# One mask instruction for four heads, and the transfer of the negated maxima asked for by GpSimd

## The chip, the cores and the metric

The kernel runs on one core of a Trainium2 chip. The metric is the device time of one execution in microseconds (us), the median over several runs. The core's engines are TensorE (PE, its weight loads shown apart as PEld), VectorE (DVE), ScalarE (ACT), GpSimd (POOL) and SyncE (SP), which here only asks for DMA transfers. Each engine takes its own instructions in order and waits on semaphores for the others.

## The reference

A block of 2048 tokens of width 512 is normalised and goes through two branches: attention in a sliding window of 256 over 32 heads of 16, and a SwiGLU feed-forward of width 1792. The feed-forward's result, through another silu, gates the attention's.

```python
def _A_ref(x, wqkv, wo):
    B, S, D = x.shape
    H = 32; Dh = D // H; W = 256
    qkv = (x @ wqkv).reshape(B, S, 3, H, Dh).transpose(2, 0, 3, 1, 4)
    q, k, v = qkv[0], qkv[1], qkv[2]
    scores = jnp.einsum("bhqd,bhkd->bhqk", q, k) * (Dh ** -0.5)
    idx = jnp.arange(S)
    mask = (idx[:, None] - idx[None, :] >= 0) & (idx[:, None] - idx[None, :] < W)
    p = softmax(jnp.where(mask[None, None], scores, -1e9))
    o = jnp.einsum("bhqk,bhkd->bhqd", p, v)
    return o.transpose(0, 2, 1, 3).reshape(B, S, D) @ wo

def _B_ref(x, w_gate, w_up, w_down):
    return (silu(x @ w_gate) * (x @ w_up)) @ w_down

xn = layernorm(A_x)
out = A_x + _A_ref(xn, A_wqkv, A_wo) * silu(_B_ref(xn, B_w_gate, B_w_up, B_w_down))
```

All tensors are float32.

## The kernel before, in words

**Precision and the two halves.** A float32 operand is split into a high part (names ending in `h`, written by ACT) and the remainder (names ending in `l`, written by POOL or DVE), and a product is the sum of three matmuls (`PAIRS`). A matmul uses 64 rows of the array, so two streams run side by side: half 0 on rows 0 to 63, half 1 on rows 64 to 127. `next_mm` gives each half its next matmul.

**Dense work.** Tokens come in 4 chunks (`NCH`) of 512. Per chunk there are units of dense work: `Proj` (`a`, queries and keys of two groups of heads), `Values` (`vp`), `GateUp` (`g`, `u`), `Down` (`d`) and `Wo` (`s`). Each has its weights loaded by SP into `wr` (two buffers), split by ACT into `wh` (L429) and by POOL into `wl` (L434), with three buffers each. All dense matmuls are at L470.

**Attention.** 32 units, 8 groups of four heads in each chunk. The four heads of a unit are two pairs `p` of one head `h` in either half of the rows. A unit's steps:

- `load_qk`: queries and keys go through DRAM (`qkd`) into `qs` and `ks`.
- `max_pair`: the scores `b` by query row (L970); DVE takes each row's maximum over the window (L978) into `m`.
- `max_turn`: PE transposes the maxima into `mt` (L1004); ACT negates them into `ms`, 16 x 128 (`neg`, L1019). A transfer of 8 KB (`put`) writes them into `qs` as a 49th row, so that the next product subtracts the maximum.
- `prob_pair(u, e, p)`: for one pair of heads and one set `e` of key blocks (`pieces`: three sets in the first chunk, four later) the transposed scores `c` (L1121), the exponential by ACT into `t`, a part of the buffer `p` (L1082), and on the blocks that the window's edge crosses a mask by POOL: L1095 on the diagonal, L1099 at the far edge. Each set has two such blocks. There are 480 masks in all, of 2 heads x 128 columns.
- `pv_visit`: the product with the values (L1158), once a unit when all its sets are masked; then `ev`, `od`, the denominators, and `o` for `Wo`.

**What sets the order.** The order of instructions on every engine is worked out when the kernel is built, by a planner that runs its own clock. `do(engine, ready, cost, fn, then, slack)` puts an instruction in a list, and `pump` issues from each list the one with the smallest `ready + slack`; `V`, `S`, `G` and `D` are DVE, ACT, POOL and the transfers that SP asks for (`dma`). A transfer's planned end is that of a stream of 230 KB/us plus `LAND` = 3.5 us, and at most eight are under way. `streams` holds the attention's steps with due marks counted in units of dense work: the maxima from u + 0.02, their transposition at u + 0.8, the probabilities from u + 1.07 in steps of 0.1, the product with the values at u + 1.89. A step is issued when it is due and its readiness function (`prob_ready`, `pv_ready`) gives a time that has come; otherwise PE gets dense matmuls. `prob_ready` asks for `ms_at[u]`, the planned arrival of the negated maxima, and for two PSUM banks; `pv_ready` asks for `pt_at`, the planned end of the masks.

`p_take` gives out pieces of the buffer `p` (`PCAP` = 6784 columns) in a ring; a unit's pieces are free again when its `pv_visit` is issued.

Of the kernel before, what the change touches and what calls it, by code (L numbers as in the profile page):

```python
# [13 lines left out]
ALU = mybir.AluOpType  # L14
# [3 lines left out]
P = 128  # L18
# [37 lines left out]
def tile_window_attention_swiglu_gate(  # L56
# [10 lines left out]
    nc = tc.nc  # L67
# [16 lines left out]
    def sb(name, shape, dtype, kind, n):  # L84
        return pers.tile(shape, dtype, name=name, tag=ring(kind, n), bufs=1)

    def f32(ap):
        return ap.bitcast(F32)

    def move(dst, src, eng=nc.sync):  # L90
        if dst.dtype == F32R:
            dst = f32(dst)
        if src.dtype == F32R:
            src = f32(src)
        eng.dma_start(dst, src)  # L95
# [11 lines left out]
    def do(e, ready, cost, fn, then=None, slack=0.5, can=None, lat=None):  # L107
        seq[0] += 1
        queue[e].append((ready + slack, seq[0], ready, cost, fn, then, can, LAT.get(e, 0.0) if lat is None else lat))
# [5 lines left out]
    def dma(ready, fn, then=None, slack=0.5, kb=256, can=None, e="D"):  # L115
        def begun_at(t):
            stream_at[0] = max(stream_at[0], t) + kb / 230.0
            done = stream_at[0] + LAND
            lanes.append(done)
            lanes.pop(0)  # L120
            if then:
                then(done)

        do(e, ready, 0.5, fn, begun_at, slack, lambda: lanes[0] <= now[0] and (can is None or can()), 0.0)
# [48 lines left out]
    def bank_time(pool, n=1):  # L173
        t = sorted(v for v in pool.values() if v is not None)
        return t[n - 1] if len(t) >= n else None

    def bank(pool, name):
        tag = min((v, k) for k, v in pool.items() if v is not None)[1]
        pool[tag] = None
        return ps.tile([P, 512], F32, name=name, tag=tag, bufs=1), tag  # L180
# [5 lines left out]
    qs = [pers.tile([P, 2, TC], F32R, name=f"q{i}") for i in range(3)]  # L186
# [168 lines left out]
    def half(r):  # L355
        return slice(R * r, R * r + R)

    def latest(times):
        times = list(times)
        return None if any(t is None for t in times) else max(times)  # L360
# [105 lines left out]
    def handover(pb):  # L466
        nc.vector.tensor_copy(pers.tile([MW, 1], F32, name="ho", tag=ring("ho", 2), bufs=1), pb[:MW, 0:1])
# [457 lines left out]
    ms_at = {}  # L925
# [72 lines left out]
    def max_turn(u, r):  # L998
        if r == 0:
            mtp[u] = [*bank(rb_free, f"mt{u}"), None]  # L1000
        pb, tag, _ = mtp[u]

        def go():
            nc.tensor.matmul(  # L1004
                pb[:MW, R * r : R * r + R], mts[u % 2][half(r), :], ident[half(r), half(r)],
                is_transpose=True, start=True, stop=True,
            )

        if r == 0:
            def after(t):  # L1010
                mtp[u][2] = t

            extra[0].append((128, go, lambda t: do("V", t, 0.09, lambda: handover(pb), after, -1.0)))
            return
        box = []

        def neg():
            box.append(sb(f"ms{u}", [16, P], F32R, "ms", 2))
            nc.scalar.activation(box[0], pb[:16, :P], AF.Copy, scale=-1.0)  # L1019

        def after_neg(t):
            rb_free[tag] = t
            dma(t, put, lambda t: ms_at.__setitem__(u, t + 1.0), -3.0, 8)

        def put():
            move(qs[u % 3][48 : 113 : 64], box[0])

        extra[1].append((128, go, lambda t: do("S", t, 0.25, neg, after_neg, -1.0)))

    def pieces(c, e):
        if c == 0:
            return ([(3, 2, 256, 0, 128, 256), (2, 2, 256, 256, 256, 512)],
                    [(0, 0, 384, 0, 0, 384)], [(1, 1, 384, 0, 0, 384)])[e]
        return ([(3, 2, 256, 0, 128, 256), (-2, 0, 256, 256, 256, 384)],
                [(-1, 0, 256, 0, 0, 256), (2, 2, 256, 256, 256, 512)],
                [(0, 0, 384, 0, 0, 384)], [(1, 1, 384, 0, 0, 384)])[e]

    pt = {}  # L1040
    pt_at = {}

# [4 lines left out]
    def p_place(n):  # L1049
        for at in (p_next[0], 0):  # L1050
            if at + n <= PCAP and all(at + n <= a or b <= at for a, b, _ in p_live):
                return at
        return None

    def p_take(h, n, u):
        at = p_place(h * n)
        p_live.append((at, at + h * n, u))
        p_next[0] = at + h * n
        return pbuf[:, at : at + h * n].rearrange("p (h n) -> p h n", h=h)

    def prob_span(u, e):
        pcs = pieces(u // NG, e)
        return min(q[4] for q in pcs), max(q[5] for q in pcs)

    def prob_ready(u, e, p):
        a, b = prob_span(u, e)
        if p_place(2 * (b - a)) is None:
            return None
        return latest([ms_at.get(u), bank_time(rb_free, 2), p_freed[0]])

# [2 lines left out]
    def prob_pair(u, e, p):  # L1073
        c = u // NG
        pcs = pieces(c, e)
        a, b = prob_span(u, e)
        t = p_take(2, b - a, u)
        pt[u, e, p] = t, a
        left = [2]

        def exp(h, pc):
            nc.scalar.activation(t[:, h, :], pc[:, a:b], AF.Exp, scale=DH ** -0.5)  # L1082

        blocks = []
        for kb, qb, w, at0, v0, v1 in pcs:
            q0 = qb + (v0 - at0) // P
            for blk in range((v1 - v0) // P):
                if q0 + blk == kb or q0 + blk == kb + 2:
                    blocks.append((v0 + blk * P, q0 + blk == kb))

        def masks():
            for at, diagonal in blocks:
                s = t[:, :, at - a : at - a + P]
                if diagonal:
                    nc.gpsimd.affine_select(  # L1095
                        s, s, [[0, 2], [1, P]], ALU.is_ge, 0.0, base=0, channel_multiplier=-1
                    )
                else:
                    nc.gpsimd.affine_select(  # L1099
                        s, s, [[0, 2], [-1, P]], ALU.is_gt, 0.0, base=0, channel_multiplier=1  # L1100
                    )

        def after(tm, tag):
            rb_free[tag] = tm
            left[0] -= 1
            if left[0] == 0:
                if blocks:
                    do("G", tm, 0.36 * len(blocks), masks, lambda t: pt_at.__setitem__((u, e, p), t), 0.0)
                else:
                    pt_at[u, e, p] = tm  # L1110

        for h in range(2):
            r = R * h
            pc, tag = bank(rb_free, f"c{u}_{e}_{2 * p + h}")

            def finished(t, h=h, pc=pc, tag=tag):
                do("S", t, 0.06 + 0.00081 * (b - a), lambda: exp(h, pc), lambda t: after(t, tag), 0.0)

            for i, (kb, qb, w, at0, _, _) in enumerate(pcs):
                def go(i=i, k0=HALO + kb * P, qb=qb, w=w, at0=at0, r=r, pc=pc):  # L1120
                    nc.tensor.matmul(  # L1121
                        pc[:, at0 : at0 + w], ks[u % 3][r : r + 49, p, k0 : k0 + P],
                        qs[u % 3][r : r + 49, p, qb * P : qb * P + w],
                        start=(i == 0), stop=True, skip_group_check=True,
                    )

                extra[h].append((w, go, finished if i == len(pcs) - 1 else None))

    def pv_ready(u, es):
        t = latest(pt_at.get((u, e, p)) for e in es for p in range(2))  # L1130
        c, g = divmod(u, NG)
        if any(vheld.get(((4 * c + kb) % VT, g // 4)) != 4 * c + kb for kb in range(-2 if c else 0, 4)):
            return None
        return None if t is None else latest([t, bank_time(rb_free, 2)])
# [268 lines left out]
    while True:  # L1403
        now[0] = max(front[0], min(clock))
        while marks and marks[-1][0] <= work[0] / PACE - LEAD:
            _, fn, a = marks.pop()
# [12 lines left out]
        if not any(extra):  # L1419
            s = work[0] / PACE - LEAD  # L1420
            for st in sorted(streams, key=lambda st: st[-1][0] if st else 1e9):
                if not st:
                    continue
                due, need, fn, a = st[-1]
# [4 lines left out]
                t = need(*a)  # L1429
# [20 lines left out]
        if os.environ.get("VIRT"):  # L1450
            u, i = stream[min(pos[0], len(stream) - 1)]
# [40 lines left out]
```

## Time and profile before

| | |
|---|---|
| three runs | 873.17, 872.02, 869.25 us; median 872.02 |
| the profiled execution | 870.93 us, of it 869.2 us from the first to the last instruction |
| granted TensorE clock | 0.999 |
| bytes moved by DMA | 139.63 MB, mean 161 GB/s |
| transfers `q<-ms` | 32, of 8 KB each, asked for by SP |
| masks on POOL | 256 at L1095 and 224 at L1099 |

A row of a group reads: line, engine, operation, output <- inputs, shapes, count | busy us, mean ns of one | idle time of the engine before them and what ended it. A row of waits reads: who waited <- for whom: us in total, times, longest. A row of the windows gives for each engine the busy us and the number of instructions, then the granted clock, the DMA engines' share and GB/s. `SPq` is SP's queue of requests. Masks that follow each other overlap a little in the records, so the distance of their starts is shorter than the time of one.

### The profile page before, as it was taken

How to read it: one execution, taken by the hardware profiler on the slowest of the kernel's cores; microseconds unless marked ns; L12 is line 12 of the kernel's file. 1: busy time of each engine (PE TensorE's matmuls, PEld its weight loads, DVE VectorE, ACT ScalarE, POOL GpSimd, SP SyncE). 2: the span in 40 equal slices, each digit the busy share in tenths (PEclk: the TensorE clock that was granted, in tenths of full speed). 3: DMA queues.
4: the chain of work that ended last, by engine and by line, in shares of the span. 5: the costliest groups of instructions: out<-in, count | busy, mean ns of one | idle time of the engine just before them, and what ended most of it. 6: DMA issues, size and time to landing. Idle time of an engine off the chain costs nothing.

```text
span 869.2 us, 30153 instructions
## 1 busy us (share of the span) xinstructions
PE 858.0 (99%) x11960; PEld 789.8 (91%) x11960; DVE 486.0 (56%) x1627; ACT 506.2 (58%) x1074; POOL 638.1 (73%) x888
## 2 busy tenths in 40 slices
PE   9999999999999999999999999999999999999997
PEld 8799999898889899989999989898999989999897
DVE  4364466655646655666555765565655566554233
ACT  4355565555665567565576666665656765566532
POOL 6576575668796776767799695676758997769774
PEclk9999999999999999999999999999999999999999
DMA  5785855466877985664767897556657779744342
GB/s 141 192 197 124 222 117 162 116 173 167 198 160 187 253 182 115 141 158 109 202 140 194 219 229 171 124 149 143 174 129 185 154 171 217 167 124 112 108 123 78
DMA packets 69489, 139.63 MB, mean 161 GB/s; under 512 B 14546, under 2 KB 23250, under 8 KB 69348
## 3 DMA queue, kind: packets, MB, share of 16 engines
q1 hardware_dynamic: 69060, 137.18, 63.9%
q8 instruction: 94, 1.54, 0.8%
q10 hardware_dynamic: 288, 0.52, 0.2%
q14 instruction: 47, 0.39, 0.2%
HBM read 107.74 MB, written 29.62 MB: 158 GB/s over the span
## 4 chain that ended last, share of the span: by engine, by line
PE 87%; DMA 8%; POOL 2%; SPq 1%; DVE 1%; issue 1%; ACT 1%; DVEq 0%; ACTq 0%; POOLq 0%
PE d L470 17%; PE u L470 15%; PE g L470 15%; PE a L470 11%; PE pv L1158 8%; PE s L470 5%; PE c L1121 5%; PE vp L470 4%; PE b L970 4%; DMA wr<-wo 2%; DMA k<-qkd 1%; POOL wl L434 1%; DMA den<-od 1%; DMA qkd<-qkl 1%; SPq L95 1%; DMA wr<-wqk 1%
## 5 line engine op out<-in xcount | busy, mean ns | idle before, releaser
L434 POOL TENSOR_TENSOR wl<-wr,wh 128x512 fp32r<-128x512 f32 (+2 forms) x258 | 306.8, 1207 | 101.1 <-ACT wh L429 91.9
L978 DVE CUSTOM_DVE_ANT_0 jk<-b,maskb 128x384 bf16<-128x384 f32 (+2 forms) x512 | 271.8, 531 | 132.5 <-PE b L970 71.5
L1082 ACT ACTIVATE p<-c 128x384 f32<-128x384 f32 (+1 forms) x480 | 208.2, 490 | 105.1 <-PE c L1121 89.0
L470 PE MATMUL d<-wh,hh 64*128 64x256 f32 x1792 | 259.3, 278 | 0.0
L470 PEld LDWEIGHTS d<-wh,hh 64*128 64x128 f32 x1792 | 227.1, 185 | 0.9 <-issue 0.6
L470 PE MATMUL d<-wl,hh 64*128 64x256 f32 x896 | 207.8, 279 | 0.0
L429 ACT ACTIVATE wh<-wr 128x512 fp32r<-128x512 f32 (+2 forms) x258 | 142.0, 594 | 65.5 <-PE d L470 16.0
L470 PE MATMUL u<-xh,wh 64*128 64x512 f32 x448 | 170.0, 396 | 0.0
L470 PE MATMUL g<-xh,wh 64*128 64x512 f32 x448 | 169.7, 395 | 0.0
L470 PE MATMUL u<-xl,wh 64*128 64x512 f32 x448 | 169.6, 396 | 0.0
L470 PE MATMUL g<-xl,wh 64*128 64x512 f32 x448 | 169.1, 395 | 0.0
L470 PE MATMUL u<-xh,wl 64*128 64x512 f32 x448 | 168.9, 395 | 0.0
L470 PE MATMUL g<-xh,wl 64*128 64x512 f32 x448 | 168.9, 395 | 0.0
L470 PEld LDWEIGHTS d<-wl,hh 64*128 64x128 f32 x896 | 154.9, 185 | 0.3
L1095 POOL TENSOR_SCALAR_AFFINE_SELECT p<-p 128x256 f32<-128x256 f32 x256 | 103.4, 408 | 57.1 <-ACT p L1082 54.0
L970 PE MATMUL b<-k,q 48*128 48x384 f32 (+1 forms) x512 | 116.6, 334 | 2.7 <-DMA k<-qkd 1.4
L1121 PE MATMUL c<-q,k 49*128 49x384 f32 (+1 forms) x704 | 111.7, 306 | 2.0 <-ACT p L1082 1.0
L1099 POOL TENSOR_SCALAR_AFFINE_SELECT p<-p 128x256 f32<-128x256 f32 x224 | 91.2, 409 | 11.4 <-ACT p L1082 9.6
L628 POOL TENSOR_TENSOR hh<-h,hh 128x512 fp32r<-128x512 f32 x56 | 72.5, 1295 | 36.4 <-ACT hh L624 30.1
L470 PE MATMUL a<-xh,wl 64*128 64x512 f32 (+1 forms) x264 | 97.0, 385 | 0.0
L470 PE MATMUL a<-xh,wh 64*128 64x512 f32 (+1 forms) x264 | 96.8, 390 | 0.0
L470 PE MATMUL a<-xl,wh 64*128 64x512 f32 (+1 forms) x264 | 96.1, 385 | 0.0
(102 smaller groups left out, 2109.6 us busy)
## 6 DMA issues: line engine op xcount, KB each, us to landing
wr<-wgu SPq DMA_DIRECT2D x112, 256.0 KB
k<-qkd SPq DMA_DIRECT2D x48, 192.0 KB
wr<-wqk SPq DMA_DIRECT2D x32, 256.0 KB
qkd<-qkh SPq DMA_DIRECT2D x32, 256.0 KB
qkd<-qkl SPq DMA_DIRECT2D x32, 256.0 KB
q<-qkd SPq DMA_DIRECT2D x64, 128.0 KB
wr<-wdn SPq DMA_DIRECT2D x32, 256.0 KB
od<-ev SPq DMA_DIRECT2D x32, 256.0 KB
```

What stands on the lines that cost most here:

```text
L95: eng.dma_start(dst, src)
L429: nc.scalar.activation(hi[0][pr, a:b], raw[pr, a:b], AF.Copy)
L434: nc.gpsimd.tensor_tensor(lo[0][pr, a:b], raw[pr, a:b], f32(hi[0][pr, a:b]), op=ALU.subtract)
L470: return nc.tensor.matmul(pb, a, b, start=first, stop=last, skip_group_check=True)
L628: nc.gpsimd.tensor_tensor(hl[:, 1, :], self.h, f32(hl[:, 0, :]), op=ALU.subtract)
L970: nc.tensor.matmul(pb[:, :w], qs[u % 3][r : r + 48, p, qb * P : (qb + 1) * P], ks[u % 3][r : r + 48, p, lo : lo + w], start=True, stop=True,)
L978: nc.vector.tensor_tensor_reduce(junk[:, :n], pb[:, :n], maskb[:, 3 * P - n :], 1.0, -3.0e38, ALU.add, ALU.max, m[:, col : col + 1],)
L1082: nc.scalar.activation(t[:, h, :], pc[:, a:b], AF.Exp, scale=DH ** -0.5)
L1095: nc.gpsimd.affine_select(s, s, [[0, 2], [1, P]], ALU.is_ge, 0.0, base=0, channel_multiplier=-1)
L1099: nc.gpsimd.affine_select(s, s, [[0, 2], [-1, P]], ALU.is_gt, 0.0, base=0, channel_multiplier=1)
L1121: nc.tensor.matmul(pc[:, at0 : at0 + w], ks[u % 3][r : r + 49, p, k0 : k0 + P], qs[u % 3][r : r + 49, p, qb * P : qb * P + w], start=(i == ...
L1158: nc.tensor.matmul(pbs[r][0][32 * j : 32 * j + 32, q0:q1], vt[half(r), (4 * c + kb) % VT, VW * (4 * g + j) : VW * (4 * g + j) + 32], t[hal ...
```

## The change

A set `e` of a unit gets one piece of the buffer `p` for all four heads (`four`), taken when its first pair is issued. Both pairs write their exponentials into it. The masks are issued once, when the fourth exponential is planned to be done, over four heads: 240 instructions of 4 x 128 columns in place of 480 of 2 x 128. The planner books 0.6 us for one instead of 0.36. `pt_at` is kept per set, not per pair.

The transfer `put` is asked for by POOL (`nc.gpsimd`) in place of SP; in the planner it is an instruction of list `G` of 1.0 us, with its arrival 2.0 us after that instruction's planned end (which includes 0.12 us), where it was the transfer's planned end plus 1.0 us.

```diff
         def after_neg(t):
             rb_free[tag] = t
-            dma(t, put, lambda t: ms_at.__setitem__(u, t + 1.0), -3.0, 8)
+            do("G", t, 1.0, put, lambda t: ms_at.__setitem__(u, t + 2.0), -3.0)
 
         def put():
-            move(qs[u % 3][48 : 113 : 64], box[0])
+            move(qs[u % 3][48 : 113 : 64], box[0], nc.gpsimd)
...
     def prob_ready(u, e, p):
         a, b = prob_span(u, e)
-        if p_place(2 * (b - a)) is None:
+        if p == 0 and p_place(4 * (b - a)) is None:
             return None
...
-        t = p_take(2, b - a, u)
+        if p == 0:
+            four[u, e] = p_take(4, b - a, u), [4]
+        whole, left = four[u, e]
+        t = whole[:, 2 * p : 2 * p + 2]
         pt[u, e, p] = t, a
-        left = [2]
...
-                s = t[:, :, at - a : at - a + P]
+                s = whole[:, :, at - a : at - a + P]
                 if diagonal:
                     nc.gpsimd.affine_select(
-                        s, s, [[0, 2], [1, P]], ALU.is_ge, 0.0, base=0, channel_multiplier=-1
+                        s, s, [[0, 4], [1, P]], ALU.is_ge, 0.0, base=0, channel_multiplier=-1
                     )
                 else:
                     nc.gpsimd.affine_select(
-                        s, s, [[0, 2], [-1, P]], ALU.is_gt, 0.0, base=0, channel_multiplier=1
+                        s, s, [[0, 4], [-1, P]], ALU.is_gt, 0.0, base=0, channel_multiplier=1
                     )
...
-                    do("G", tm, 0.36 * len(blocks), masks, lambda t: pt_at.__setitem__((u, e, p), t), 0.0)
+                    do("G", tm, 0.6 * len(blocks), masks, lambda t: pt_at.__setitem__((u, e), t), 0.0)
                 else:
-                    pt_at[u, e, p] = tm
+                    pt_at[u, e] = tm
...
-        t = latest(pt_at.get((u, e, p)) for e in es for p in range(2))
+        t = latest(pt_at.get((u, e)) for e in es)
```

More of the change, by code (lines that the diff above doesn't have):

```diff
@@ L1041, in tile_window_attention_swiglu_gate @@
     pt_at = {}
+    four = {}
     pbuf = pers.tile([P, PCAP], F32, name="p")
```

## The prediction

> **What bounds the kernel now.** First the page's head: the span, the busy time of each engine and the chain of work that ended last.
>
> ```profile
> span 869.2 us, 30153 instructions
> PE 858.0 (99%) x11960; PEld 789.8 (91%) x11960; DVE 486.0 (56%) x1627; ACT 506.2 (58%) x1074; POOL 638.1 (73%) x888
> PE 87%; DMA 8%; POOL 2%; SPq 1%; DVE 1%; issue 1%; ACT 1%; DVEq 0%; ACTq 0%; POOLq 0%
> ```
>
> TensorE has 858.0 of 869.2 us; the change touches none of its 11960 matmuls. Only 11.2 us of the span are without a matmul, and POOL holds 2% of the chain. So the question is which of those 11 us, and which stretches with only one of the two row halves at work, hang on masks or on the transfer of the maxima. The second view is the waits of PE and of its weight loads:
>
> ```profile
> PE b L970 <- DMA k<-qkd: 1.4, 1, 1.4
> PE c L1121 <- ACT p L1082: 1.0, 1, 1.0
> PE c L1121 <- DMA q<-ms: 0.8, 1, 0.8
> ...
> PEld pv L1158 <- issue: 4.2, 14, 0.4
> PEld c L1121 <- ACT p L1082: 3.4, 7, 1.5
> PEld pv L1158 <- POOL p L1099: 2.0, 6, 0.4
> ```
>
> The columns are total, times and longest. The transfer that the change moves has held PE once, for 0.8 us. The masks hold the start of `pv` by at most 0.4 us at a time, mostly less than the matmul then running. The third view cuts the span into stretches (PE busy, weight loads, DVE, ACT, POOL, clock, DMA share):
>
> ```profile
> 230.00:260.00 30.00, 28.73 (x427) 24.64 (x423) 14.48 (x50) 16.71 (x36) 24.93 (x32) 1.00 0.76 172
> 280.00:305.00 25.00, 24.35 (x368) 21.79 (x367) 14.94 (x51) 12.24 (x27) 17.05 (x26) 1.00 0.94 248
> 470.00:500.00 30.00, 29.20 (x426) 27.50 (x423) 17.66 (x61) 17.72 (x38) 23.18 (x34) 1.00 0.84 216
> 500.00:690.00 190.00, 190.00 (x2808) 175.77 (x2807) 115.05 (x382) 119.82 (x259) 139.63 (x207) 1.00 0.68 162
> 690.00:720.00 30.00, 28.91 (x369) 24.29 (x371) 15.02 (x48) 18.05 (x37) 27.38 (x37) 1.00 0.77 179
> ```
>
> Between 500 and 690 us PE has no gap at all. The gaps lie in four short stretches: 1.27 + 0.65 + 0.80 + 1.09 = 3.81 us; the other 7.4 us are start and end, which the change doesn't reach. In the four stretches the weight loads too run below their share of 500 to 690 (175.77 / 190 = 0.925): 30 x 0.925 - 24.64 = 3.1, 25 x 0.925 - 21.79 = 1.3, 30 x 0.925 - 27.50 = 0.3, 30 x 0.925 - 24.29 = 3.5, together 8.2 us. That is the bound on what better order there could return. The chain through the worst of them:
>
> ```profile
> 690.13 0.29 POOL p L1099
> 690.43 0.36 POOL p L1095
> 690.79 0.36 POOL p L1099
> 691.15 2.49 POOL gp L757 x2
> 693.64 1.24 POOL wl L434
> ...
> 697.95 10.90 DMA wr<-wo
> ```
>
> POOL's backlog, 1.0 us of masks in it, comes ahead of the weight split that frees the buffer for the load of `wo`; the load itself takes 10.9 us beside a DMA share of 0.77. The larger piece is transfer, not POOL.
>
> **The change, part by part.**
>
> *Masks.* Three widths of the same POOL operation:
>
> ```profile
> L1095 POOL TENSOR_SCALAR_AFFINE_SELECT p<-p 128x256 f32<-128x256 f32 x256 | 103.4, 408 | 57.1 <-ACT p L1082 54.0 <-DMA q<-qkd 1.4 <-DMA k<-qkd 0.8
> L1099 POOL TENSOR_SCALAR_AFFINE_SELECT p<-p 128x256 f32<-128x256 f32 x224 | 91.2, 409 | 11.4 <-ACT p L1082 9.6 <-DMA wr<-wdn 1.6
> L202 POOL TENSOR_SCALAR_AFFINE_SELECT maskb<-maskb 128x384 f32<-128x384 f32 x1 | 0.5, 505 | 0.1
> masks.py:199 POOL TENSOR_SCALAR_AFFINE_SELECT ident<-ident 128x128 f32<-128x128 f32 x1 | 0.3, 293 | 0.1
> ```
>
> 128, 256 and 384 columns take 293, 408 and 505 ns, so 512 take about 605 (the last step, 97 to 100, added). In the chain above the masks follow each other every 0.36 us, 0.05 less than they last; 512 columns are then 0.56. 480 x 0.36 = 172.8 us become 240 x 0.56 = 134.4: 38.4 us less on POOL. Bounds for a wide mask: 0.36 (cost all fixed) to 0.72 (no saving).
>
> The masks of the first pair now wait for the second pair's exponentials, so after the fourth exponential 2 x 0.56 = 1.12 us follow in place of 0.72: `pv` of a unit can be ready 0.40 us later. Every `pv` place in PE's order is set by the planner from the planned end of the masks (0.72 before, 1.2 now), so PE's order moves along and other matmuls stand ahead of `pv`. Bounds: from -2.0 us (the six waits on L1099 gone) to 24 units x 0.2 = +4.8 (half of the 0.40 felt as a wait each time). I take 0, because the planned 1.2 is above my 1.12, while the planned 0.72 was equal to the measured. On POOL what is queued behind a mask, the weight splits at L434, waits for the fourth exponential with it. That wait stands already in the row of L1095 (54.0 us before 256 masks) and PE's waits name no `wl`; 0.
>
> *The transfer of the negated maxima.* It leaves SP and becomes an instruction on POOL. Nothing in the trace shows POOL asking for a transfer. The rows of SP:
>
> ```profile
> L95 SPq DMA_DIRECT2D q<-ms x32: 553/600/1432, 52.1 to 787.7; - x32
> SPq L95 <- POOL wl L434: 134.9, 60, 6.3
> SPq L95 <- ACT ms L1019: 18.6, 10, 3.9
> ```
>
> SP loses 32 x 0.600 = 19.2 us of asking and 18.6 us in which it stood for the ACT result with weight loads queued behind it. None of this was on PE's path except through the stretches above; what is late next for SP is the 134.9 us of waits for POOL's weight splits, which stay. For POOL I bound one request from 0.6 us (SP's row) to 1.3 (POOL's own 128x512 operations, 2.49 for two in the chain). 32 of them: 19 to 42 us. With the masks POOL's work changes by -38.4 + 19 = -19 up to -38.4 + 42 = +3 us in 638. So POOL is hardly relieved; and the planner, at 0.72 per pair of blocks before, 1.2 and 1.0 now, books 16 x 0.36 = 5.76 us per later unit before and 8 x 0.6 + 1.0 = 5.8 after. What waits behind the request on POOL is again a weight split or mask; it stands for ACT's `ms`, 0.25 us after `mt`.
>
> How soon must the transfer land? Two units, the first without a wait, the second the one with 0.8:
>
> ```profile
> L1019 ACT ACTIVATE ms<-mt x1: 249/249/249, 118.9 to 118.9; 16x128 fp32r<-16x128 f32 x1
> L1121 PE MATMUL c<-q,k x8: 276/278/279, 124.4 to 125.8; 49*128 49x256 f32 x8
> L1019 ACT ACTIVATE ms<-mt x1: 268/268/268, 231.3 to 231.3; 16x128 fp32r<-16x128 f32 x1
> L95 SPq DMA_DIRECT2D q<-ms x1: 602/602/602, 231.9 to 231.9; - x1
> L1121 PE MATMUL c<-q,k x8: 277/278/384, 239.8 to 240.3; 49*128 49x256 f32 x8
> ```
>
> In the first, `c` starts 124.4 - 118.9 - 0.25 = 5.3 us after `ms` and waits for nothing. In the second the transfer, behind others in SP's queue and asked for at 231.9, ended PE's wait at about 239.8: 7.3 us from the end of its issue. The planner used to allow the queue, 3.5 us and 1.0; it now allows 1.0 + 0.12 + 2.0 = 3.1 us after POOL is free. Where the unit's due mark does not hold `c` back, PE reaches it at least 3.5 + 1.0 - 3.1 = 1.4 us sooner. In a queue of its own the transfer has nothing of its queue ahead, so the 7.3 us case should go: -0.8. The other side: each `c` could wait for a landing later than 3.1 us. Bounds from -0.8 to 32 x 0.5 = +16 (half a microsecond late in every unit); I take -0.8, because the due mark, 0.27 of a unit after that of the maxima, keeps most units near the 5.3 us seen. The Trainium skill (DMA: Bandwidth & Descriptors, Anatomy of one DMA) gives a POOL-asked transfer about 2.0 us plus bytes over 436 GB/s, 2.02 us for 8 KB as an estimate, and by it no `c` would wait and the sum would stay the same; no run here shows that yet.
>
> *The four stretches.* What is left of 3.81 - 0.8 = 3.0 us: bounds -3.0 and 0. Of the 18.9 us of chain from 690.0 to 708.9, 1.0 is masks, which shrink by 0.56 / 0.72: -0.22 a stretch, -0.9 for four; I take -0.5.
>
> *Sum.* 0 + 0 - 0.8 - 0.5 = -1.3 us. The profiled execution was 870.93 us (span 869.2 and 1.73 around it), so 869.6; the median of the three runs, 872.02, is 1.09 above it: 870.7 us. Within 0.5% means 867.7 to 876.4, about what a measurement of this kernel can tell from no change.
>
> **The rivals.**
>
> *Faster: the four stretches close up.* SP is free of 37.8 us of requests and waits, `c` comes 1.4 us sooner, POOL's splits come sooner, so the load of `wo` starts earlier. For it: the chain passes through POOL's backlog and SP there. Against it: 10.9 of 18.9 us are the load itself, and no byte is removed. It gives between the 3.8 us of gaps and 3.8 + 8.2 / 2 = 7.9 us: about 872.0 - 6 = 866 us.
>
> *Slower: `c` waits for the new transfer.* PE takes instructions in order, so every late landing stops both halves. Place: the first `c` of each unit, with L1082's ACT and POOL's masks queued behind. It decides from 4.4 / 32 = 0.14 us mean wait a unit; at 0.25 us it is 32 x 0.25 = 8 us, 880 us. For it: the planned distance falls from above 5 us to 3.1, and POOL is 73% busy when the request comes. Against it: PE waits of this kind are 0.8 us in all now, and the due mark adds distance.
>
> *Slower: VectorE holds the request back.* If POOL must stand still while a VectorE operation runs, a request at a random moment meets one with 56% and loses half of it:
>
> ```profile
> L978 DVE CUSTOM_DVE_ANT_0 jk<-b,maskb 128x384 bf16<-128x384 f32 (+2 forms) x512 | 271.8, 531 | 132.5 <-PE b L970 71.5
> L1095 POOL TENSOR_SCALAR_AFFINE_SELECT p<-p x256: 396/407/434, 59.2 to 810.5; 128x256 f32<-128x256 f32 x128
> ```
>
> 0.56 x 0.53 / 2 = 0.15 us a unit, 4.8 us in all without slack: 877 us. Against it: of 256 masks beside the same VectorE work none took over 434 ns, so no such hold of half a microsecond is in the trace. The rule stands in the Trainium skill (SBUF — State Buffer, SBUF: two separate sides), which ties it to VectorE operations that use both port pairs.
>
> *The change doesn't relieve POOL at all* (wide mask 0.72 or request above 1.3 us). By the bounds above that moves PE by less than 0.5%; it is inside the forecast.
>
> **How the numbers follow.** No measurable change 0.50; faster through the stretches 0.28; slower through waits of `c` 0.17; through VectorE 0.05. The range from 864 to 880 us takes in the faster rival down to 8 us and the slower one up to its 0.25 us a unit, leaving about 0.1 on either side; the forecast's own range is 868 to 875.
>
> **What would show it.** Right: 240 masks near 605 ns, POOL's busy time lower by about 48 us (480 x 0.408 - 240 x 0.605 = 50) before the requests are counted; PE still 99% busy; no row in which PE `c` waits for `q<-ms`, or one below 1 us; gaps still in the four stretches. Wrong, to the slow side: a row of PE `c` waiting for `q<-ms` with many times. Wrong, to the fast side: PE busy all through the stretches, weight loads at 0.92 of them. A change of PE's rate between 500 and 690 us would mean that the new order itself pairs the halves differently, which I cannot see from here.

## The result: slower by 0.49%

The changed kernel takes 874.55 us in the median of 14 runs (868.26 to 878.12), the kernel before 869.12 us in 14 runs on the same chip (866.66 to 873.17). The ratio is 1.0049 with a 95% interval of 1.0030 to 1.0069, some 4.3 us. It is not the quotient of the two medians, which would be 1.0062 (5.4 us); by both the changed kernel is slower. The two profiled executions hide this: that of the kernel before (870.93 us) lies 1.8 us above its median, that of the changed kernel (871.36) 3.2 us below its own, so the two spans look alike. What PE waits for differs.

The head of the page after, and the waits of PE and of its weight loads (total us, times, longest):

```profile
span 869.3 us, 29842 instructions
PE 854.1 (98%) x11960; PEld 793.0 (91%) x11960; DVE 485.6 (56%) x1627; ACT 506.9 (58%) x1074; POOL 624.4 (72%) x680
PE 86%; DMA 8%; POOL 3%; issue 1%; ACT 1%; DVE 0%; SPq 0%; ACTq 0%; POOLq 0%; DVEq 0%
```

```profile
PE c L1124 <- DMA q<-ms: 7.2, 7, 1.9
PE b L970 <- DMA k<-qkd: 1.2, 1, 1.2
...
PEld c L1124 <- issue: 7.9, 5, 2.2
PEld pv L1161 <- issue: 4.0, 13, 0.4
PEld pv L1161 <- POOL p L1102: 1.8, 5, 0.4
```

The row `PE c <- DMA q<-ms` was 0.8 us in one place and is now 7.2 us in seven, 7.2 / 32 = 0.23 us a unit. The 7.9 us of "issue" of the weight loads of `c` are the same time seen a second time: they stand at five of the seven places. The product with the values waits for its masks as long as before. The transfer's own rows, with the time from the request to the landing in the last line:

```profile
L1019 ACT ACTIVATE ms<-mt x32: 249/267/268, 51.7 to 786.8; 16x128 fp32r<-16x128 f32 x32
L95 POOL DMA_DIRECT2D q<-ms x32: 575/575/779, 52.6 to 788.3; - x32
...
  PE c L1124: 7.2, 7
...
DMA to landing us min/median/max: 1.7/4.1/7.4
```

The request is quick, 0.575 us. The landing has a median of 4.1 us after the request's start and a maximum of 7.4. The planner allows 1.0 + 0.12 + 2.0 = 3.1 us. PE's order leaves more than that, but less than it did. From the end of `ms` to the unit's first `c`, read unit by unit from the traces, were 7.6 us in the median and 5.3 at least in the kernel before; now they are 6.2 and 4.2. The transfer lands 4.5 us after `ms` in the median and 7.7 at most. The seven waits are the units in which it lands after PE has come to `c`. One of the seven places as a chain (start, us, what):

```profile
379.36 0.43 POOL p L1102
379.78 0.18 issue
379.96 1.22 POOL wl L434
381.18 6.41 DMA q<-ms
387.58 0.14 issue
387.72 0.51 PE c L1124 x4
```

`mt` was done at 379.2 and ACT's `ms` at 379.9; the request stood behind a weight split on POOL until 381.18, the transfer took 6.41 us, and `c` started in the moment after it. Where the gaps are now (PE, weight loads, DVE, ACT, POOL, clock, DMA share):

```profile
40.00:230.00 190.00, 185.90 (x2453) 174.57 (x2451) 110.58 (x410) 109.83 (x233) 127.22 (x136) 1.00 0.65 161
230.00:260.00 30.00, 29.54 (x361) 26.87 (x359) 17.02 (x59) 19.00 (x41) 26.73 (x28) 1.00 0.77 172
280.00:305.00 25.00, 24.27 (x386) 22.46 (x385) 14.41 (x51) 12.29 (x27) 16.73 (x19) 1.00 0.89 241
470.00:500.00 30.00, 29.59 (x425) 27.61 (x423) 19.30 (x64) 18.52 (x40) 22.56 (x25) 1.00 0.85 218
690.00:720.00 30.00, 30.00 (x376) 28.09 (x375) 17.46 (x59) 20.50 (x43) 28.97 (x30) 1.00 0.79 198
```

The four stretches have 0.46 + 0.73 + 0.41 + 0.00 = 1.6 us of gaps in place of 3.81. Between 40 and 230 us 4.1 us have opened, where the kernel before had PE busy for all but 0.12 us:

```profile
40.00:230.00 190.00, 189.88 (x2488) 175.82 (x2486) 113.50 (x419) 112.90 (x239) 133.59 (x181) 1.00 0.65 164
```

The masks and the requests on POOL after the change:

```profile
L1098 POOL TENSOR_SCALAR_AFFINE_SELECT p<-p 128x512 f32<-128x512 f32 x128 | 81.5, 640 | 56.0 <-ACT p L1085 53.0
L1102 POOL TENSOR_SCALAR_AFFINE_SELECT p<-p 128x512 f32<-128x512 f32 x112 | 71.7, 640 | 15.1 <-ACT p L1085 15.0
L95 POOL DMA_DIRECT2D q<-ms x32 | 19.1, 596 | 8.0 <-ACT ms L1019 7.0 <-DMA wr<-wv 0.4 <-issue 0.2
```

### The profile page after: what moved, and what is told of

It reads as the page before. It is cut to its first block, busy times and chain, and to the rows that moved or that the text cites. A ratio compares the mean times of both kernels' runs of the same rounds, so it can differ in the third digit from the quotient of the medians.

```text
span 869.3 us, 29842 instructions
## 1 busy us (share of the span) xinstructions
PE 854.1 (98%) x11960; PEld 793.0 (91%) x11960; DVE 485.6 (56%) x1627; ACT 506.9 (58%) x1074; POOL 624.4 (72%) x680
## 4 chain that ended last, share of the span: by engine, by line
PE 86%; DMA 8%; POOL 3%; issue 1%; ACT 1%; DVE 0%; SPq 0%; ACTq 0%; POOLq 0%; DVEq 0%
PE d L470 17%; PE u L470 16%; PE g L470 16%; PE a L470 9%; PE pv L1161 7%; PE c L1124 6%; DMA q<-ms 5%; PE s L470 5%; PE b L970 4%; PE vp L470 4%; POOL wl L434 2%; DMA q<-qkd 1%; DMA wr<-wqk 1%; PE warm L236 1%; DMA wr<-wv 1%
## 5 line engine op out<-in xcount | busy, mean ns | idle before, releaser
L470 PE MATMUL d<-wl,hh 64*128 64x256 f32 x896 | 205.0, 279 | 0.0
L470 PE MATMUL u<-xh,wl 64*128 64x512 f32 x448 | 166.2, 395 | 0.0
L470 PE MATMUL u<-xl,wh 64*128 64x512 f32 x448 | 166.1, 395 | 0.0
L470 PE MATMUL u<-xh,wh 64*128 64x512 f32 x448 | 166.0, 395 | 0.0
L470 PE MATMUL g<-xl,wh 64*128 64x512 f32 x448 | 165.8, 395 | 0.0
L470 PE MATMUL g<-xh,wh 64*128 64x512 f32 x448 | 165.3, 394 | 0.0
L470 PE MATMUL g<-xh,wl 64*128 64x512 f32 x448 | 165.0, 395 | 0.0
L1098 POOL TENSOR_SCALAR_AFFINE_SELECT p<-p 128x512 f32<-128x512 f32 x128 | 81.5, 640 | 56.0 <-ACT p L1085 53.0
L970 PE MATMUL b<-k,q 48*128 48x384 f32 (+1 forms) x512 | 113.7, 333 | 1.2 <-DMA k<-qkd 1.2
L1124 PEld LDWEIGHTS c<-q,k 49*128 49x128 f32 x704 | 83.7, 185 | 13.1 <-issue 7.9
```

The costliest lines, as they stand in the source:

```text
L470: return nc.tensor.matmul(pb, a, b, start=first, stop=last, skip_group_check=True)
L970: nc.tensor.matmul(pb[:, :w], qs[u % 3][r : r + 48, p, qb * P : (qb + 1) * P], ks[u % 3][r : r + 48, p, lo : lo + w], start=True, stop=True,)
L1098: nc.gpsimd.affine_select(s, s, [[0, 4], [1, P]], ALU.is_ge, 0.0, base=0, channel_multiplier=-1)
L1124: nc.tensor.matmul(pc[:, at0 : at0 + w], ks[u % 3][r : r + 49, p, k0 : k0 + P], qs[u % 3][r : r + 49, p, qb * P : qb * P + w], start=(i == ...
```

## The experiments

Every ratio is to the kernel before, run on the same chip at the same time, with its 95% interval. "Order" is the order of instructions that the planner writes; any number that it books changes it.

### Each half alone

`e1_masks_only`: the masks of the change, the transfer as before.

```diff
-            do("G", t, 1.0, put, lambda t: ms_at.__setitem__(u, t + 2.0), -3.0)
+            dma(t, put, lambda t: ms_at.__setitem__(u, t + 1.0), -3.0, 8)
-            move(qs[u % 3][48 : 113 : 64], box[0], nc.gpsimd)
+            move(qs[u % 3][48 : 113 : 64], box[0])
```

> Only the four-head masks; the transfer of the maxima is asked for by SP and planned as in the kernel before. Theory A (the loss is PE waiting at c for the transfer, because its planned arrival of 3.1 us after the ACT result is shorter than the 4.5 us median of the changed kernel): ratio 0.996 to 1.001 to the kernel before, PE waits for q<-ms below 1 us. Theory B (the loss comes from the wide masks, which hold POOL until the fourth exponential, and from the new order that they give): ratio 1.003 to 1.007 without waits for q<-ms.

1.0034 (1.0012 to 1.0057), waits for `q<-ms` 1.0 us. Taken alone this speaks for theory B; e5, e10 and e11 below give lower values for the same instructions in other orders.

`e2_transfer_only`: the same two lines of the change alone, with two-head masks.

> Only the transfer is asked for by GpSimd, with the changed kernel's planned arrival; the masks stay two heads wide. Theory A: ratio 1.003 to 1.008, PE waits for q<-ms of 5 to 12 us in 5 to 10 places. Theory B: ratio 0.998 to 1.002.

1.0139 (1.0116 to 1.0162), 12.1 us and more than either expectation. The wait of PE, and the transfer's landing:

```profile
PE c L1121 <- DMA q<-ms: 8.6, 6, 2.6
```

```profile
DMA to landing us min/median/max: 1.7/4.0/7.9
```

PE's wait is 8.6 us, 3.5 less than the loss. The granted clock (the number before the DMA share) shows most of the rest. Two of the waits, of 2.1 us up to 58.2 and of 2.6 us up to 244.6, are each followed by a stretch at half the clock:

```profile
58.50:61.90 3.40, 3.40 (x30) 3.40 (x28) 0.00 (x0) 1.91 (x5) 2.20 (x5) 0.50 0.36 76
246.30:249.70 3.40, 3.40 (x22) 3.09 (x20) 1.52 (x6) 1.17 (x4) 3.40 (x6) 0.51 0.03 5
```

Half of 3.4 us, twice, is another 3.4 us.

The halves do not add up to the whole, so the order that comes out of each booking has to be held fixed to price the instructions.

### The instructions in the old order

`e5_masks_old_order`: the planner books as before; the program writes the wide mask at the second of the two old places. PE's order is identical.

```diff
         def masks():
+            due[0] -= 1
+            if due[0]:
+                return
             for at, diagonal in blocks:
-                s = t[:, :, at - a : at - a + P]
+                s = whole[:, :, at - a : at - a + P]
```

> Every engine's order as in the kernel before: the planner still books two masks of two heads, but the program writes one mask over four heads at the second of the two places. The transfer stays on SP. Masks alone with a new order measured 1.0034 (1.0012 to 1.0057). Theory O (the loss of the masks alone is the new order of PE, not the wide masks): ratio 0.997 to 1.001. Theory M (waiting for the fourth exponential and the longer last mask cost PE time): ratio 1.002 to 1.006, with longer waits of pv for POOL.

0.9971 (0.9950 to 0.9992): in this order the wide masks cost PE nothing, theory M is out. How much they gain is less sure: the medians, 868.21 and 869.47 us, differ by 0.14% only.

`e6_transfer_old_order`: the kernel before, only `move(..., nc.gpsimd)`, the planner's booking unchanged.

> PE's order exactly as in the kernel before, two-head masks; only the request for the maxima stands on POOL in place of SP. Transfer alone with its own planned arrival measured 1.0139. Theory A (the distance from the request to c in PE's order costs the time, not who asks): ratio 0.998 to 1.003, PE waits for q<-ms below 2 us. Theory G (the request on POOL or its landing is itself slow enough): ratio 1.006 to 1.014.

1.0004 (0.9984 to 1.0024): who asks is not what costs. In the old order the same request from POOL is in time in all units but one, though it lands no sooner: 4.6 us after `ms` in the median (4.5 in the changed kernel). What differs is the distance from `ms` to `c`, 7.6 us in the median here and 6.2 there. PE's wait, then the landing after the request:

```profile
PE c L1121 <- DMA q<-ms: 1.0, 1, 1.0
```

```profile
DMA to landing us min/median/max: 1.8/3.6/7.1
```

`e9_both_old_order`: both edits together.

> Both instructions of the change (wide masks, request on POOL) in exactly the order of the kernel before. If the two effects add (0.9971 for the masks, 1.0004 for the request): 0.996 to 0.999. If the request on POOL and the late wide mask hinder each other there: 1.001 to 1.004. The distance to 1.0049 is what the new order costs.

1.0018 (0.9996 to 1.0039). Above the sum of the two, with intervals that meet. By the middle values 0.31 of the change's 0.49% are the order; the two intervals overlap, so this is a rough figure.

### Is another order worse by itself?

`e7_replan`: the kernel before with `0.37 * len(blocks)` booked in place of 0.36, no other edit. `e12_masks_replan`: wide masks in that order.

> A control: the kernel before, with the same instructions, but the planner books 0.37 us for a mask instead of 0.36, which gives PE another order. Theory O: the order before is a favourable one among many, and another order alone costs 2 to 5 us: ratio 1.002 to 1.006. Otherwise: 0.999 to 1.001.

> Wide masks written at the second of the two old places, in the order that 0.37 us for a mask gives (the control with two-head masks measured 0.9983). If the gain of the wide masks does not depend on the order: 0.9971 x 0.9983 = 0.9954, so 0.993 to 0.998. If it was bound to the order before: 0.998 to 1.001.

0.9983 (0.9964 to 1.0002) and 0.9986 (0.9965 to 1.0007). This new order is not worse by itself. And in it the wide masks bring nothing by the middle values (0.9986 against 0.9983); the intervals are too wide to say that the gain in e5 belongs to its order alone.

`e10_masks_booked_036` and `e11_masks_booked_064`: e1 with `0.36 * len(blocks)` or `0.64 * len(blocks)` in place of 0.6.

> Masks only, planned as one task after the fourth exponential, but booked at 0.36 us for one instead of 0.6; SP asks as before. Theory S (the long booking after the fourth exponential places pv and the next unit worse): ratio 0.996 to 1.000. Theory P (every order that plans one task after the fourth exponential is worse): 1.002 to 1.005 as with 0.6 (1.0034).

> Masks only, as one task, booked at 0.64 us (what one lasts) instead of 0.6: only another order. Theory S: 1.003 to 1.006. Theory P: 1.002 to 1.005. Theory C (which order comes out is chance, with a spread of some 0.3%): away from 1.0034 by more than 0.2%, on either side.

1.0015 (0.9998 to 1.0032) and 0.9998 (0.9978 to 1.0018), beside 1.0034 with 0.6. In e10, where 0.36 is too little, `pv` stands too early and waits 8.9 us for masks (6.2 us with "issue" in the kernel before, 8.9 + 3.9 here), and yet it is not the slowest. The three do not follow the booking, which fits theory C, an order's chance of some 0.3%. That e1's 1.0034 is such a chance is likely, not shown: its profiled execution was among its fastest (867.55 us of 867.12 to 875.50) and has no wait that would explain its median.

### The distance from the transfer to `c`

`e8_sp_early_mark`: the kernel before, with `t - 0.4` in place of `t + 1.0` in `after_neg`. SP asks, the masks are two heads wide.

> The kernel before, with SP asking and two-head masks, but the planner is told that the maxima arrive 1.4 us earlier, so that c stands nearer to the transfer. Theory A: PE waits for q<-ms of 5 to 12 us and a ratio of 1.004 to 1.012, without GpSimd having any part in it. Theory G: ratio 0.999 to 1.003.

1.0071 (1.0043 to 1.0099), `PE c <- DMA q<-ms` 6.3 us in 3 places, 4.0 the longest. The distance from `ms` to `c` is 6.2 us in the median, as in the changed kernel. A nearer `c` costs time with no part of GpSimd in it; what e8's order costs beside the wait was not measured apart.

`e3_late_mark`: the whole change with `t + 4.5` in place of `t + 2.0`.

> The whole change, but the planner is told that the maxima arrive 4.5 us instead of 2.0 us after the request's planned end, so that c stands later in PE's order. Theory A: PE waits for q<-ms fall from 7.2 us to below 2 us and the ratio to the kernel before to 0.996 to 1.001. Theory B: ratio stays at 1.003 to 1.007.

1.0039 (1.0018 to 1.0059): the waits fall to 2.3 us, but the ratio hardly moves. Taken alone this contradicts theory A; the runs further down settle it for the changed kernel's own mark, and for the late mark in part.

`e4_act_asks`: the whole change, with ACT asking.

```diff
-            do("G", t, 1.0, put, lambda t: ms_at.__setitem__(u, t + 2.0), -3.0)
+            do("S", t, 0.6, put, lambda t: ms_at.__setitem__(u, t + 2.0), -3.0)
-            move(qs[u % 3][48 : 113 : 64], box[0], nc.gpsimd)
+            move(qs[u % 3][48 : 113 : 64], box[0], nc.scalar)
```

> The whole change, but ACT asks for the transfer in its own queue, right behind the operation that writes the maxima (planned 0.6 us on ACT and 2.0 us to arrival). Theory A1 (a transfer in a queue of its own lands late because the 16 DMA engines are busy with SP's packets): landing has a median of 3 to 4 us after the request as with GpSimd (4.1), PE waits of 5 us or more, ratio 1.002 to 1.008. Theory A2 (GpSimd's way of asking is what is slow): landing 1.5 to 2 us, waits below 1 us, ratio 0.996 to 1.001.

1.0237 (1.0207 to 1.0268), far above either expectation. The profile tells no median of the landings for this queue; `PE c <- DMA q<-ms` is 14.5 us in 5 places, 5.3 the longest. The chain through the longest:

```profile
427.68 11.48 DMA r<-rd
...
439.24 4.31 DMA q<-ms
443.56 0.14 issue
443.69 0.80 PE c L1124 x4
```

`ms` was done at 432.0, but the request started at 439.24 only: ACT's queue stood until a transfer that SP had asked for (`r<-rd`) had landed. Ahead of the 3.6 us wait the request is late by 4.2 us. So a large part of e4's waits comes from late requests on ACT, not from late landings, and e4 does not decide between A1 and A2.

The changed kernel's own trace says more on A1. Three requests fall into times in which SP moves next to nothing; three of the slowest landings do not. These are the stretches from request to landing (the DMA share is the number before the last):

```profile
332.00:333.90 1.90, 1.90 (x54) 1.00 (x58) 0.84 (x2) 1.85 (x4) 1.87 (x3) 1.00 0.03 5
406.00:407.80 1.80, 1.80 (x56) 1.14 (x60) 0.18 (x1) 0.00 (x0) 1.78 (x3) 1.00 0.03 5
765.00:766.80 1.80, 1.80 (x85) 1.41 (x68) 0.00 (x0) 0.10 (x1) 1.78 (x3) 1.00 0.03 5
95.60:103.00 7.40, 5.73 (x119) 4.51 (x116) 1.38 (x6) 2.35 (x4) 2.91 (x3) 1.00 0.80 265
381.20:387.60 6.40, 4.99 (x107) 3.79 (x91) 2.57 (x7) 1.20 (x2) 1.84 (x3) 1.00 0.68 231
716.10:723.20 7.10, 7.10 (x139) 6.23 (x142) 3.67 (x12) 2.32 (x4) 5.05 (x6) 1.00 1.04 233
```

The landing takes 1.7 to 1.8 us at a share of 0.03 and 6.4 to 7.4 at 0.68 to 1.04. The share is not all of it: the request at 359.6 took 3.3 us at 0.10.

Why e4's loss, 20.6 us, is larger than its waits, the granted clock around the longest shows:

```profile
430.00:438.00 8.00, 8.00 (x147) 6.74 (x145) 2.82 (x10) 1.93 (x6) 5.04 (x6) 1.00 0.64 186
438.00:443.50 5.50, 0.43 (x5) 0.11 (x1) 1.31 (x4) 2.15 (x4) 4.20 (x4) 0.88 0.72 261
443.50:450.00 6.50, 6.31 (x51) 6.34 (x53) 2.12 (x7) 2.74 (x7) 3.73 (x5) 0.58 0.23 63
450.00:458.00 8.00, 8.00 (x128) 8.00 (x126) 5.11 (x19) 5.63 (x13) 5.33 (x7) 1.00 0.84 151
```

After 5.3 us of waiting TensorE has 0.58 of its clock for 6.5 us: another 6.5 x 0.42 = 2.7 us. After the waits of 3.8 and 3.6 us it has 0.76 from 243 to 250 us and 0.50 from 497 to 503: another 1.7 and 3.0 us.

### The wait taken away in the same order

`f1_after_no_max`: the changed kernel, instruction for instruction in its order, but `c` reads 48 rows and not the 49th, so that it depends on no transfer. `f2_before_no_max`: the same edit in the kernel before.

```diff
-                        pc[:, at0 : at0 + w], ks[u % 3][r : r + 49, p, k0 : k0 + P],
-                        qs[u % 3][r : r + 49, p, qb * P : qb * P + w],
+                        pc[:, at0 : at0 + w], ks[u % 3][r : r + 48, p, k0 : k0 + P],
+                        qs[u % 3][r : r + 48, p, qb * P : qb * P + w],
```

> Every engine's order as in the changed kernel (1.0049), but c reads 48 rows and not the 49th with the maxima, so that nothing waits for the transfer (the scores go into the exponential without their maximum subtracted; the transfer is still made). Theory A (the loss is PE's waits for the transfer): ratio 0.996 to 1.000, no waits for q<-ms. Theory C (the new order is a worse one by chance, whatever the transfer does): 1.002 to 1.006.

> The same in the order of the kernel before (c reads 48 rows, no subtraction of the maximum), as a control of what the missing wait and row are worth there: 0.8 us of waits go, ratio 0.997 to 1.000.

1.0009 (0.9989 to 1.0029) in the changed order, from 1.0049 (1.0030 to 1.0069); 0.9999 (0.9982 to 1.0015) in the old one. The missing row itself is worth nothing, the missing wait 0.4%. What f1 keeps, 0.09%, is not clear of nothing.

`f3_booked_064`: the whole change with `0.64 * len(blocks)`; `f4_booked_064_late`: that and `t + 4.5`; `g2_booked_no_max`: f3 with 48 rows.

> The whole change with 0.64 us booked for a wide mask in place of 0.6, which with SP asking measured 0.9998 against 1.0034: another order with the same short distance to c. Theory A: waits for q<-ms of 5 to 10 us again and a ratio of 1.003 to 1.008. Theory C: anywhere from 0.997 to 1.004, without a tie to the waits.

> The whole change with 0.64 us booked for a wide mask and the maxima planned to arrive 4.5 us after the request's planned end, in place of 2.0. Theory A: waits for q<-ms below 2.5 us, ratio 0.997 to 1.002, and below that of the same kernel with 2.0. Theory C: no tie to the mark.

> The order of the whole change with 0.64 us booked (1.0082), with c reading 48 rows (no maximum subtracted): a second order with the short distance and its wait taken away. Theory A: ratio 0.998 to 1.003. Theory C: above 1.005.

1.0082 (1.0053 to 1.0110), 1.0044 (1.0022 to 1.0065) and 0.9999 (0.9973 to 1.0025). In a second order, too, the loss goes with the wait. Its size can't be read from f3's profile: the profiled execution is f3's fastest (867.78 us), and PE's waits for `q<-ms` in it are 4.1 us in 5 places, below the 5 to 10 expected. By the middle values the later mark takes off about half of the loss: 4.5 us are still less than some landings, since f4 has this wait of PE and these landings:

```profile
PE c L1124 <- DMA q<-ms: 1.7, 2, 1.4
```

```profile
DMA to landing us min/median/max: 1.7/3.8/7.3
```

`g1_late_no_max`: e3 with 48 rows.

> The order of the kernel with the late mark (4.5 us, 1.0039), with c reading 48 rows so that nothing waits for the transfer (no maximum subtracted). If what is left there are still late transfers: ratio 0.998 to 1.001. If it is the order or the request on POOL: 1.003 to 1.005.

1.0016 (0.9991 to 1.0040), from 1.0039: some of what is left with the late mark is the wait again, but the intervals overlap, so the rest stays open.

## Why the prediction was wrong

Forecast was 870.7 us, 1.3 us below the median of the three runs known then, as no measurable change; measured is 4.3 us more than the kernel before. The time lies in the range; the direction is that of the second rival.

- **The step that failed** is the one on the transfer, "I take -0.8, because the due mark, 0.27 of a unit after that of the maxima, keeps most units near the 5.3 us seen". In place of -0.8 us PE waited 7.2 us in the profiled execution, and by f1 the wait is worth 0.4% of 869 us, 3.5 us. Two things in this step were wrong.
  - *The distance.* 5.3 us were seen in one unit, which is the shortest of the old trace's 32; the median was 7.6. The due mark did not keep it: the median fell by 1.4 us to 6.2, by as much as the planned arrival did.
  - *The landing.* "In a queue of its own the transfer has nothing of its queue ahead, so the 7.3 us case should go": it did not go, landings of up to 7.4 us stayed (7.1 in e6), and the long ones fall where SP keeps the DMA engines busy (1.7 to 1.8 us at a share of 0.03, up to 7.4 above 0.6). No run takes SP's transfers away, so this rests on the 32 requests of one trace. The Trainium skill says the same (DMA: Bandwidth & Descriptors, Issuing engines are not separate DMA queues: DMAs of every issuing engine run on the same 16 DMA engines and interleave). This rule, not the one I cited, bore on the change. The one I cited (the Trainium skill, DMA: Bandwidth & Descriptors, Anatomy of one DMA, about 2.0 us) agrees with the 1.7 to 1.8 us beside an idle SP and not with the median of 4.1. My upper bound of +16 us held; within it I chose the wrong end.
- **The rival "`c` waits for the new transfer"** was right in mechanism and place, and nearly in its size: it was to decide from 0.14 us a unit; 0.23 were measured. It had 0.17.
- **VectorE holding the request back** is not seen: the 32 requests last 575 ns in the median and 779 at most, so none was lengthened by as much as one of VectorE's 0.53 us. A hold ahead of a request's start would not show in these times.
- **Masks**: 640 ns where I had 605. POOL's busy time on the page fell by 638.1 - 624.4 = 13.7 us. With the 19.1 us of requests, the lower end of 19 to 42, the masks took about 33 us less. I had 38.4 in the sum and 50 as the sign; the 50 adds up durations (42 with the measured 640), and so counts twice the time in which masks overlap. The 0 for `pv` held: its waits were 6.2 us and are 5.8.
- **The four stretches** lost 3.81 - 1.60 = 2.2 us of gaps, the 0.8 and 0.5 of the sum and a little more. The faster rival was at work there, and is outweighed by the 4.1 us between 40 and 230 us.
- **"The new order itself pairs the halves differently, which I cannot see from here"**: the same instructions, wide masks with SP asking, ranged over five orders from 0.9971 (e5) to 1.0034 (e1), wider than the effect forecast. I gave that no term; it belonged into the range, not into the sum.

The lowest ratio of all is e5, wide masks in the old order with SP asking, 0.9971 (0.9950 to 0.9992). In e12's order the same masks gained nothing by the middle values, so I would not count on it.

## What to carry to other kernels

Where a planner or a list fixes PE's order, a number that it books for a transfer is a change of its own: price an edit once with the order held fixed, and once with the wait taken away in the new order. Book a small transfer by the slow end of its landing times under the load of that kernel, not by its time on an idle chip, and don't expect a queue of its own to get past the other queues' packets. Take the distance that an order leaves from the median and the shortest of all units, not from one of them. A gain on an engine that is not the bound (33 us of POOL here) was worth 0 to 0.3%.

## What the runs showed of the hardware that was not expected

- An 8 KB transfer inside the core, asked for by GpSimd, takes 1.7 to 7.4 us to land in one and the same kernel, 1.7 to 1.8 where the DMA share is 0.03, while the request itself takes GpSimd 0.575 us.
- A mask over 128, 256, 384 and 512 columns takes GpSimd 293, 408, 505 and 640 ns: the last step is larger (135 ns) than the two before.
- Waits of 2.1 and 2.6 us were each followed by 3.4 us at half of TensorE's clock (e2), a wait of 5.3 us by 6.5 us at 0.58 of it (e4), so these waits cost half to four fifths more than they last. After the changed kernel's waits of at most 1.9 us the profiled execution shows no lower clock.
